# Moving half of a weight load behind the values of batch 1, and four half sums of weights into tile 1

## The chip, the core and the metric

The kernel runs on one core of a Trainium2 chip. A core has several engines that each work through a queue of their own: TensorE (PE in the profile) multiplies matrices, with a separate row, PEld, for loading the stationary operand; VectorE (DVE) and ScalarE (ACT) do elementwise work; GpSimd (POOL) does elementwise work more slowly and also issues most of the DMA transfers here; SyncE (SP) issues the others. An instruction starts when the one before it on its engine has gone and the semaphores that it waits for have been raised. The metric is the device time of one execution in microseconds (us).

## The reference

Attention in which keys and values are first averaged over groups of eight positions, followed by a two-layer network with a SiLU between its layers:

```python
k_p = k.reshape(B, H, Sp, pool, D).mean(axis=3)      # pool 8: 576 positions become 72
v_p = v.reshape(B, H, Sp, pool, D).mean(axis=3)
scores = scale * np.matmul(q, k_p.transpose(0, 1, 3, 2))
attn = softmax(scores)
x = np.matmul(attn, v_p)      # then to (4608 tokens, 512)
h = x @ w_in                  # 512 -> 2048
g = h * (1.0 / (1.0 + np.exp(-h)))
out = g @ w_out               # 2048 -> 512
```

There are 8 batches, 8 heads, 576 positions and a head dimension of 64. Inputs and output are float32; the kernel multiplies in bf16.

## The kernel before

The 4608 tokens are worked through in nine tiles of 512 (`NT`). For each tile the kernel needs the attention output `xT` and then two layers. Because 576 positions are not 512, a tile reaches into the next batch: tile 0's second half and tile 1 need keys and values of batch 1. While tile t is in its layers, the attention for tile t + 1 is worked in between.

From tile 1 on both layers (in tile 0 a part of the first) use Strassen's scheme, in the Winograd form: a 2 x 2 block product with seven multiplications instead of eight. It needs sums of blocks of both operands. Sums of w_in's blocks are `unit_weight_sum` (into `w_sum1`), of `xT` `unit_x_sum` (into `x_sum`), of w_out's blocks `weight_sum` (L841, into `w_sum`) and of the hidden layer `hidden_sum`. `weight_sum(n, i)` makes sum n (0 to 3) for half i of the rows; one call is one VectorE instruction that reads two operands from SBUF (L845, 128 x 1024 bf16). All eight calls have to be done before tile 1's second layer, which starts at 61.4 us. Tile 0 multiplies its second layer directly (`second_product`, L801): "m1:8-12" multiplies row block 1 of the hidden layer with blocks 8 to 11 of w_out's 16. It needs the DMA of just those blocks.

In tiles with the scheme a first-layer group (a, b, c, d) has products 1 to 7. "a6" is two steps of two matmuls each, followed by what `behind` (L916) does: after product 1 a copy of bank A into bank B, after product 5 a copy of bank E into f32, after product 6 the sum of bank B and that copy into bank E (L925, VectorE). Product 7 then adds into bank B, so it waits until that sum has read it.

The order is written by hand. A string such as `FIRST` (L1172, for tile 0) or `ONE` (L1177, for tile 1) gives TensorE's products in order; each is a number of steps, and `spread` (L682) issues other work at given steps: `at(86, select_v, 1, j)` puts the call behind step 86. Tile 0 has 108 steps. What stands under the same engine keeps the order in which it was issued, so a later number moves a call back in its engine's queue. The calls of tile 0 that matter here:

- `slot_sums` for "v" (L339): six VectorE additions (L346) that add the eight positions of a group for batch 1's values, in two parts, `raw` into `v5`. They wait for the three DMAs of `load_slots(nc.gpsimd, 1, "v", ...)`.
- `select_v` (L377): small matmuls that bring these sums into heads (`v_ps`, L386); `copy_v` (L411) copies them out on ScalarE; `turn_v` moves them with DMAs on SyncE.
- `denominators` and `reciprocals` (TensorE, then four ScalarE activations), `numerators` (L525, L501: TensorE), and `x_half` (L534, L537: four VectorE products into `xT`).
- `load_half_2`, `load_v_last`, `spread_keys`: loads and one small GpSimd operation for later tiles.

Tile 1 starts on VectorE with its four `unit_x_sum` (L735). `behind_x_sums` (L737) is a copy of one column of the last of these on GpSimd (`gate`, L738): GpSimd works in order, so what stands behind the copy there begins only after the x sums. Behind it stand six additions of batch 2's keys (`slot_sums` "k" with `eng=nc.gpsimd`), issued at tile 1's step 0.

All loads of w_in, w_out, q, and the k and v of batch 1 and later (but for `load_v_last`) go through one queue that GpSimd issues. `load_w_out(c, c1)` (L1052) loads eighths c up to c1 of w_out, two without c1; an eighth is two of the 16 blocks, 256 KB as it lands.

Of the kernel before, what the change touches and what calls it, by code (L numbers as in the profile page):

```python
# [36 lines left out]
def kernel(  # L37
# [9 lines left out]
    nc = tc.nc  # L47

    B, H, S, D = q.shape
# [144 lines left out]
    def last_rows(bs):  # L194

        lasts[bs] = mid.tile([128, 2, 2 * PH], FP32, tag="r_raw", bufs=1, name="r_raw")
        return lasts[bs][:, : len(bs)]
# [123 lines left out]
    def load_slots(eng, b, name, i0, i1, half=None):  # L321
        es = slice(0, RE) if half is None else slice(half * RE // 2, (half + 1) * RE // 2)
        src = (k if name == "k" else v)[b].rearrange("h (sp p) d -> (h sp) (p d)", p=POOL)
        src = src[:, es]
        how = dict(accum_op=ALU.add) if half else {}
        tiles = row_tiles[name]
        w = es.stop - es.start
        if i0 == SLOTS:
            eng.dma_start(
                out=tiles[1][:REST, SLOTS - SA, :w], in_=src[128 * SLOTS :], **how  # L330
            )
        else:
            j = i0 // SA
            eng.dma_start(
                out=tiles[j][:, i0 - SA * j : i1 - SA * j, :w],
                in_=src[128 * i0 : 128 * i1].rearrange("(i r) e -> r i e", r=128), **how
            )
# [714 lines left out]
    def load_w_out(c, c1=None):  # L1052
        cs = slice(c * KG // 8, (c + 2 if c1 is None else c1) * KG // 8)
        nc.gpsimd.dma_start(out=w_out_sb[:, cs, :], in_=w_out_r[:, cs, :])
# [73 lines left out]
    load_q(1, halves=True)  # L1128
    load_q_part(1, 0, 2 * UT - QI)
    load_w_out(3, 4)  # L1130
    load_w_out(4)
    load_slots(nc.gpsimd, 1, "v", 0, 3)
    load_slots(nc.gpsimd, 1, "v", 3, 4)
    load_slots(nc.gpsimd, 1, "v", 4, 5)
    load_w_out(6)
    row_masks(True)
    load_q_part(1, 2 * UT - QI, QI)
# [18 lines left out]
    def load_half_2(name, half):  # L1156
# [14 lines left out]
    )  # L1171
    FIRST = (  # L1172
        "p0.1 p2.1 c1 p4.1 c5 p6.1 c6 c2 d1 d5 c7 c3 d6 d2 c4 cs m0:0-2 d7 d3 m0:2-4 m1:0-1 ds d4"
        " m1:1-4 m2:0-4 m0:4-6 m1:4-6 m2:4-6 m0:6-8 m1:6-8 m2:6-8 m3:0-8 m0:8-12 m1:8-12 m2:8-12 m3:8-12 m0:12-16"
        " m1:12-16 m2:12-16 m3:12-16"
    )
    ONE = "a1 b1 a5 b5" + FOUR[FOUR.index(" a6"):].replace("o2:0-2", "o2:0-3").replace("o2:2-8", "o2:3-8")  # L1177
# [1 line left out]
    for t in range(NT):  # L1179
        a = t + 1  # L1180
        if t == 0:
            f = []

            def at(s, fn, *args, **kw):
                f.append((s, lambda: fn(*args, **kw)))

            for n in (0, 2, 1, 3):
                at(0, unit_x_sum, 0, n)
            for y, y_at in ((2, 0), (3, 18), (1, 66)):
                for n in range(4):  # L1190
                    at(y_at + n, unit_weight_sum, y, y + 1, n)
            for n in range(3):
                at((39, 42, 44)[n], slot_sums, "k", 0, levels=(n,))
            at(46, slot_sums, "k", 1)
            for a in range(2):
                at(50, q_transpose, 1, a, 0, QI - UT)
            for j in range(2):
                at(53, select_k, 1, j)
            at(53, copy_k, 1, slice(0, 2), nc.scalar.copy)
            for i0, i1 in ((0, SA), (SA, SLOTS), (SLOTS, SLOTS + 1)):  # L1200
                at(47, load_slots, nc.gpsimd, 2, "k", i0, i1)
            at(47, load_q, 2)
            for a in range(2):
                at(55 + a, q_transpose, 1, a, QI - UT, UT)
            at(52, attn_tables)
            for i in range(PW):
                at(63 + i, weight_sum, 0, i)
            for n in (1, 2, 3):
                at(74, weight_sum, n, 0)
            for j in range(2):  # L1210
                at(75 + j, slot_sums, "v", j)
                at(86, select_v, 1, j)
            at(86, copy_v, 1, 0, nc.scalar.copy, H)
            at(88, turn_v, 1)
            for n in (1, 2):
                at(91, weight_sum, n, 1)
            at(84, load_half_2, "v", 0)
            at(48, lambda: nc.gpsimd.memset(last_rows((1, 2))[:, :, :1], 0.0))
            at(80, load_v_last, 1, 2)
            at(84, spread_keys, 1, nc.gpsimd)  # L1220
            at(61, scores_half, 1, 0)
            at(73, scores_half, 1, 1)
            for n in range(2):
                at(84, denominators, 1, n)
                at(84, reciprocals, 1, n)
            at(92, numerators, 1, 0)
            at(92, numerators, 1, 1)
            for n in range(2):
                at(92, x_half, 1, n)
            at(93, moe_tables)  # L1230
            tile_products(0, FIRST, f)
            continue

        order = ORDER.get(t, FOUR if t < NT - 1 else BARE)
        if t == NT - 1:
            order = order.replace("P4 Q4", "R4 S4")
        o = 0
        f = []

        def at(s, fn, *args, **kw):  # L1240
            f.append((s, lambda: fn(*args, **kw)))

        def late(s, fn, *args, **kw):
            at(s + o, fn, *args, **kw)

        if t == 1:
            for n in (0, 2, 1, 3):
                at(0, unit_x_sum, 1, n)
            at(0, behind_x_sums)
        late(43, hidden_sum, 2, 0, 4)  # L1250
        late(53, hidden_sum, 2, 4, 8)
        late(64 if t < NT - 1 else 57, hidden_sum, 0, 0, 4)
        late(64 if t < NT - 1 else 62, hidden_sum, 1, 0, 4)
        late(65, hidden_sum, 0, 4, 8)
        late(66, hidden_sum, 1, 4, 8)
        late(76, hidden_sum, 3, 0, 8)
        if a < B:
            if t == 1:
                at(8, weight_sum, 3, 1)
                for j in range(2):  # L1260
                    at(0, slot_sums, "k", j, eng=nc.gpsimd)
                    at(42, select_k, 2, j)
                    at(43, copy_k, 2, j, nc.scalar.copy)
                    at(69, slot_sums, "v", j, halves=True)
                at(1, load_half_2, "v", 1)
                at(48, spread_keys, 2)
                at(84, pick_v, 2)
                for n in "kv":
                    at(3, load_one, 3, n)
                at(37, last_sums, 1, 2, eng=nc.vector, levels=(0,))  # L1270
                at(44, last_sums, 1, 2, eng=nc.vector, levels=(1, 2))
                at(46, load_v_last, 3)
                at(86, last_values, 1, 2, eng=nc.vector)
                for n in "kv":
                    at(5, load_rest, 3, n)
                at(33, load_q, 3)
            else:
                at(0, behind_x_sums)
                at(0, pool_k, a)
                if a + 1 < B:  # L1280
                    at(0, load_one, a + 1, "k")
                at(1, pool_v, a)
                if a + 1 < B:
                    at(1, load_one, a + 1, "v")
                    at(1, load_v_last, a + 1)
                    at(3, load_rest, a + 1, "k")
                    at(4, load_rest, a + 1, "v")
                    at(33, load_q, a + 1)
                at(34, k_transpose, a)
                at(35, spread_keys, a)  # L1290
        if t < NT - 1:
            tail = QI - UT + 2 * t
            for n in range(2):
                at((22, 32)[n], q_transpose, a, n, 0, tail)
                if tail < UT:
                    at((47, 55)[n], q_transpose, a, n, tail, UT)
            late(63, attn_tables)
            late(63, scores, a)
            late(88, sums_and_values, a)
            late(89, x_part, a, 0)  # L1300
            late(89, moe_tables)
            late(95, x_part, a, 1)
        if t < NT - 1:
            for n in (0, 2, 1, 3):
                late(102 if (t, n) == (1, 0) else 105, unit_x_sum, t + 1, n)
        tile_products(t, order, f, last=t == NT - 1)
# [28 lines left out]
```

## Time and profile before

| | us |
|---|---|
| three runs | 269.28, 269.98, 276.65 |
| median | 269.98 |
| the profiled execution, its own time | 269.99 |
| its span (first to last instruction) | 268.1 |
| second layer of tile 0: first product to last (L809) | 28.1 to 49.2 |
| tile 1's first product | 49.0 |

| DMA queue | packets | MB | share of 16 engines' span |
|---|---|---|---|
| issued by GpSimd (q0) | 22480 | 25.97 | 51.5% |
| hardware queues (q1) | 8384 | 11.87 | 16.6% |

The span lies 1.9 us below the execution's own time; sums are made against the latter. The granted TensorE clock is full over the whole span, and the DMA engines are busy in almost all of the first 50 us: in the stretches of 2 us from 16 to 44 us the mean share of the engines is 1.03 to 1.25 (packets overlap), with 195 to 397 GB/s. In a row of the timeline the columns are start, duration, engine, line, operation, what it writes and reads, shapes and count; in brackets the engine's idle time before it and what ended that. The ends of matmuls are modelled and overlap the next ones' starts, so a matmul's pace is read from starts.

### The profile page before, as it was taken

What the parts mean: (1) busy time and instruction counts of PE and PEld (TensorE: products, weight loads), DVE (VectorE), ACT (ScalarE), POOL (GpSimd) and SP (SyncE); (2) the same over time, 40 slices, a digit from 0 to 9 for tenths busy, and PEclk for the clock granted to TensorE, in tenths of its full rate; (3) what the DMA queues carried; (4) which work ended last, traced back from release to release, by engine and by line L of the source; (5) the groups of instructions that cost most, each with busy time, mean ns of one, the idle gap of its engine ahead of it and who ended that gap; (6) DMA issues with size and microseconds to landing.
All of it is one profiled execution on the core that took longest, in us unless ns stands there. A gap on an engine that the chain in (4) does not pass through costs nothing.

```text
span 268.1 us, 7721 instructions
## 1 busy us (share of the span) xinstructions
PE 261.0 (97%) x3143; PEld 212.4 (79%) x3148; DVE 209.8 (78%) x378; ACT 182.1 (68%) x319; POOL 114.9 (43%) x155
## 2 busy tenths in 40 slices
PE   8999998999999999999999999999999999999994
PEld 4468643788888888888888888888888887888883
DVE  4878978789797959895988598859886887686862
ACT  1579866788658865876587658765876677667700
POOL 8664745591638713872297229684900000000000
PEclk9999999999999999999999999999999999999999
DMA  7999999669698796579666956699500150015004
GB/s 208 284 205 288 205 284 299 204 141 202 134 163 223 205 184 129 134 173 182 131 154 161 182 121 155 148 177 125 120 12 0 37 125 0 2 32 127 2 0 157
DMA packets 31330, 38.97 MB, mean 145 GB/s; under 512 B 9760, under 2 KB 21536, under 8 KB 31296
## 3 DMA queue, kind: packets, MB, share of 16 engines
q0 software_dynamic: 22480, 25.97, 51.5%
q1 hardware_dynamic: 8384, 11.87, 16.6%
q10 hardware_dynamic: 432, 0.66, 0.7%
q8 instruction: 24, 0.39, 0.6%
q14 instruction: 10, 0.08, 0.1%
HBM read 37.88 MB, written 9.44 MB: 177 GB/s over the span
## 4 chain that ended last, share of the span: by engine, by line
PE 83%; DMA 13%; DVE 1%; issue 1%; POOL 0%; POOLq 0%
PE o_psB L910 16%; PE u_psB L891 16%; PE o_psA L910 11%; PE o_psE L910 11%; PE u_psE L891 10%; PE u_psA L891 10%; DMA raw<-in_k_dram 4%; DMA raw<-in_v_dram 4%; DMA w_in_sb<-in_moe_w_in_dram 3%; DMA q_bf<-in_q_dram 2%; PE o_ps L809 2%; PE sc_ps L575 2%; PE den_ps L604 1%; PE nu_ps L629 1%; DVE raw L346 1%
## 5 line engine op out<-in xcount | busy, mean ns | idle before, releaser
L891 PEld LDWEIGHTS <-w_sum 128*128 128x128 bf16 x544 | 52.8, 98 | 6.5
L910 PEld LDWEIGHTS <-h_sum 128*128 128x128 bf16 x512 | 48.8, 98 | 7.7 <-issue 0.4
L891 PEld LDWEIGHTS <-w_in_sb 128*128 128x128 bf16 x408 | 39.9, 98 | 4.8
L910 PEld LDWEIGHTS <-h_T 128*128 128x128 bf16 x384 | 36.9, 98 | 5.2 <-issue 0.4
L891 PE MATMUL u_psA<-xT,w_in_sb 128*128 128x256 bf16 x272 | 40.5, 273 | 0.0
L891 PE MATMUL u_psB<-x_sum,w_sum 128*128 128x256 bf16 x272 | 40.3, 273 | 0.1
L910 PE MATMUL o_psA<-w_out_sb,h_T 128*128 128x256 bf16 x256 | 32.1, 273 | 0.0
L910 PE MATMUL o_psB<-w_sum,h_sum 128*128 128x256 bf16 x256 | 31.8, 273 | 0.0
L925 DVE TENSOR_TENSOR u_psE<-u_psB,p 128x512 f32<-128x512 f32 x34 | 23.7, 697 | 8.7 <-PE u_psB L891 5.0
L929 ACT ACTIVATE h_T<-u_psE 128x512 bf16<-128x512 f32 x34 | 20.3, 597 | 10.2 <-PE u_psE L891 9.9
L942 DVE TENSOR_TENSOR c<-u_psB,p 128x512 f32<-128x512 f32 x34 | 23.2, 682 | 3.2 <-PE u_psB L891 2.1
L670 DVE TENSOR_TENSOR xT<-nu_ps,rec 128x512 bf16<-128x512 f32 x28 | 18.0, 682 | 9.8 <-ACT rec L654 9.8
L920 DVE COPY u_psB<-u_psA 128x512 f32<-128x512 f32 x30 | 20.8, 698 | 4.7 <-PE u_psA L891 4.2
L929 ACT ACTIVATE h_T<-u_psB 128x512 bf16<-128x512 f32 x34 | 20.4, 599 | 5.5 <-PE u_psB L891 5.5
L929 ACT ACTIVATE h_T<-u_psA 128x512 bf16<-128x512 f32 x34 | 20.5, 602 | 4.6 <-PE u_psA L891 4.5
L923 ACT COPY p<-u_psE 128x512 f32<-128x512 f32 x34 | 20.1, 595 | 4.0 <-PE u_psE L891 4.0
L211 POOL DMA_DIRECT2D v_raw<-in_v_dram x20 | 18.3, 1023 | 8.6 <-DMA v_raw<-in_v_dram 8.5
L929 ACT ACTIVATE h_T<-c 128x512 bf16<-128x512 f32 x34 | 21.7, 637 | 0.2 <-DVE c L942 0.2
L834 DVE TENSOR_TENSOR h_sum<-h_T 128x1024 bf16<-128x1024 bf16 x32 | 21.6, 679 | 0.2 <-ACT h_T L929 0.2
L834 DVE TENSOR_TENSOR h_sum<-h_T,h_sum 128x1024 bf16<-128x1024 bf16 (+1 forms) x24 | 20.7, 863 | 0.2
L891 PE MATMUL u_psB<-xT,w_sum 128*128 128x256 bf16 x136 | 20.4, 273 | 0.0
L891 PE MATMUL u_psE<-x_sum,w_in_sb 128*128 128x256 bf16 x136 | 20.4, 273 | 0.0
(125 smaller groups left out, 462.6 us busy)
## 6 DMA issues: line engine op xcount, KB each, us to landing
out_dram<-o_sb SPq DMA_DIRECT2D x128, 64.0 KB
raw<-in_k_dram POOLq DMA_DIRECT2D x10, 576.0 KB, 8.4
v_raw<-in_v_dram POOLq DMA_DIRECT2D x20, 256.0 KB, 7.5
q_bf<-in_q_dram POOLq DMA_DIRECT2D x5, 576.0 KB, 9.2
w_in_sb<-in_moe_w_in_dram POOLq DMA_DIRECT2D x8, 256.0 KB, 7.8
r_raw<-in_v_dram SPq DMA_DIRECT2D x28, 64.0 KB
raw<-in_v_dram POOLq DMA_DIRECT2D x2, 768.0 KB, 8.8
w_out_sb<-in_moe_w_out_dram POOLq DMA_DIRECT2D x3, 512.0 KB, 10.8
```

Of the source, the lines that this page charges most:

```text
L211: nc.gpsimd.dma_start(out=batches[b]["v_raw"][KM * g : KM * (g + 1)], in_=source(b, "v")[:KM, 4 * g : 4 * (g + 1), PH * half : PH * (half ...
L575: nc.tensor.matmul(sc[s][KM * g : KM * (g + 1), cs], lhsT=kz[b % 2][rows, g, c, :KM], rhs=qT[rows, g, us, :, c], start=(n == 0 and c == 0) ...
L670: nc.vector.tensor_mul(out=xT[:, 2 * g : 2 * g + 2, x_cols(t, f)], in0=st["nu"][g][f], in1=inv[:, f : f + 1, :].broadcast_to([128, 2, NQ]),)
L809: nc.tensor.matmul(ps["m", m], lhsT=h_T[:, g, m * 128 : (m + 1) * 128], rhs=w_out_sb[:, g, :], start=(g == 0), stop=(g == KG - 1),)
L834: nc.vector.tensor_tensor(out=h_sum[n][:, k0:k1, :], in0=get(a), in1=get(b), op=op)
L891: nc.tensor.matmul(ps[y, BANK[n]][:, u, :], lhsT=w[:, kk, 128 * u : 128 * (u + 1)], rhs=x[:, kk, :], start=n in (1, 5) and u == 0 and kk == 0,
L910: nc.tensor.matmul(o_bank(n, c), lhsT=left(n, kt, c), rhs=w[:, kt, :], start=n in (1, 5) and kt == 0 and c == 0, stop=kt == KQ - 1, skip_g ...
L920: (acopy if t == 0 or (t == 1 and y in (0, 1)) else vcopy)(ps[y, "B"], ps[y, "A"])
L923: acopy(f32[y], ps[y, "E"])
L925: tt(out=ps[y, "E"], in0=ps[y, "B"], in1=f32[y], op=add)
L929: nc.scalar.activation(h_T[:, g : g + 2, j * NQ : (j + 1) * NQ], src, func=AF.Silu)
L942: tt(out=c22, in0=ps[y, "B"], in1=f32[y], op=add)
```

## The change

Half of w_out's third quarter, eighth 5 (blocks 10 and 11), is loaded behind batch 1's values instead of before them, as a DMA of its own. Tile 0's second layer takes blocks 8 and 9 for all four row blocks first, and then blocks 10 and 11. Of the weight sums, `weight_sum(1, 0)` and `(2, 0)` go from step 74, ahead of the value sums, to step 89, behind them; `(3, 0)` and `(1, 1)`, `(2, 1)` leave tile 0 (steps 74 and 91) and stand with `(3, 1)` in tile 1 at step 1, behind the x sums. The selection of values, its copy and the moves behind it are issued four steps later, the denominators and reciprocals one step earlier, the numerators, products into `xT` and the table load behind them two steps later.

```diff
     load_w_out(3, 4)
-    load_w_out(4)
+    load_w_out(4, 5)
     load_slots(nc.gpsimd, 1, "v", 0, 3)
     load_slots(nc.gpsimd, 1, "v", 3, 4)
     load_slots(nc.gpsimd, 1, "v", 4, 5)
+    load_w_out(5, 6)
     load_w_out(6)
...
-        " m1:1-4 m2:0-4 m0:4-6 m1:4-6 m2:4-6 m0:6-8 m1:6-8 m2:6-8 m3:0-8 m0:8-12 m1:8-12 m2:8-12 m3:8-12 m0:12-16"
+        " m1:1-4 m2:0-4 m0:4-6 m1:4-6 m2:4-6 m0:6-8 m1:6-8 m2:6-8 m3:0-8 m0:8-10 m1:8-10 m2:8-10 m3:8-10 m0:10-12 m1:10-12 m2:10-12 m3:10-12 m0:12-16"
...
-            for n in (1, 2, 3):
-                at(74, weight_sum, n, 0)
+            for n in (1, 2):
+                at(89, weight_sum, n, 0)
             for j in range(2):
                 at(75 + j, slot_sums, "v", j)
-                at(86, select_v, 1, j)
-            at(86, copy_v, 1, 0, nc.scalar.copy, H)
-            at(88, turn_v, 1)
-            for n in (1, 2):
-                at(91, weight_sum, n, 1)
+                at(90, select_v, 1, j)
+            at(90, copy_v, 1, 0, nc.scalar.copy, H)
+            at(92, turn_v, 1)
...
             for n in range(2):
-                at(84, denominators, 1, n)
-                at(84, reciprocals, 1, n)
-            at(92, numerators, 1, 0)
-            at(92, numerators, 1, 1)
+                at(83, denominators, 1, n)
+                at(83, reciprocals, 1, n)
+            at(94, numerators, 1, 0)
+            at(94, numerators, 1, 1)
             for n in range(2):
-                at(92, x_half, 1, n)
-            at(93, moe_tables)
+                at(94, x_half, 1, n)
+            at(95, moe_tables)
...
             if t == 1:
-                at(8, weight_sum, 3, 1)
+                at(1, weight_sum, 3, 0)
+                for n in (1, 2, 3):
+                    at(1, weight_sum, n, 1)
```

## The prediction

> **What bounds the kernel now.** I read the busy shares first.
>
> ```profile
> PE 261.0 (97%) x3143; PEld 212.4 (79%) x3148; DVE 209.8 (78%) x378; ACT 182.1 (68%) x319; POOL 114.9 (43%) x155
> ```
>
> TensorE (PE) has work for all but some 7 us of the 268.1 us span. Whatever stops it adds to the end, and what removes a stop takes off the end; nothing later has slack to give back. The row of the granted clock is full throughout. Next, the waits between 41 and 50 us, the end of tile 0 (us in total, times, longest):
>
> ```profile
> PE v_ps L386 <- DVE v L346: 1.2, 2, 1.0
> ```
>
> This is the stop at which the change is made. TensorE's order around it and in the start of tile 1 (start, us, engine, line, what):
>
> ```profile
> 41.08 0.60 PE L809 MATMUL o_ps<-w_out_sb,h_T 128*128 128x512 bf16 x2
> 41.86 0.41 PE L386 MATMUL v_ps<-v,shifts 128*128 128x64 bf16 x8 [0.18 <-DVE v L346]
> 43.24 0.28 PE L386 MATMUL v_ps<-v,shifts 128*128 128x64 bf16 x4 [0.97 <-DVE v L346]
> ...
> 44.74 1.07 PE L501 MATMUL nu_ps<-es,vp 72*32 72x64 bf16 x48
> 45.97 3.18 PE L809 MATMUL o_ps<-w_out_sb,h_T 128*128 128x512 bf16 x14 [0.16 <-issue]
> 48.99 1.04 PE L891 MATMUL u_psA<-xT,w_in_sb 128*128 128x256 bf16 x8
> ...
> 52.49 0.60 PE L891 MATMUL u_psB<-x_sum,w_sum 128*128 128x256 bf16 x4
> ```
>
> Counted by starts, the stop is 1.4 to 1.5: two products from 41.08 fill until 41.5, eight small matmuls from 41.86 until 42.1 (the recorded ends hold a drain of 0.17). The row at 52.49 is product a7, which adds into the bank that VectorE's (DVE's) sum at 51.45 reads. On VectorE:
>
> ```profile
> 39.86 1.55 DVE L346 TENSOR_TENSOR raw<-raw 128x768 f32<-128x768 f32 x2 [0.94 <-DMA raw<-in_v_dram]
> ...
> 45.27 2.48 DVE L537 TENSOR_TENSOR xT<-nu_ps,rec 128x512 bf16<-128x512 f32 x4 [0.88 <-PE nu_ps L501]
> ...
> 49.39 0.68 DVE L845 TENSOR_TENSOR w_sum<-w_out_sb,w_sum 128x1024 bf16<-128x1024 bf16 x1
> 51.45 0.70 DVE L925 TENSOR_TENSOR u_psE<-u_psB,p 128x512 f32<-128x512 f32 x1 [1.38 <-PE u_psB L891]
> ```
>
> VectorE began batch 1's value sums when the load landed, so that stop starts in the DMA queue. Its DMAs (name, KB, us from issue to landing) were issued at 29.16, 31.27 and 31.81:
>
> ```profile
> w_out_sb<-in_moe_w_out_dram POOLq DMA_DIRECT2D x1, 512.0 KB, 7.8
> ...
> raw<-in_v_dram POOLq DMA_DIRECT2D x1, 128.0 KB, 9.6
> ...
> w_out_sb<-in_moe_w_out_dram POOLq DMA_DIRECT2D x1, 512.0 KB, 11.3
> ```
>
> They land one after the other: w_out's third quarter at 37.0, the last values at 40.9, w_out's last quarter at 43.1. Last, GpSimd (POOL) at the start of tile 1, and the gate copy's six durations (ns, least, median, most):
>
> ```profile
> 49.54 0.58 POOL L738 COPY gate<-x_sum 128x1 bf16<-128x1 bf16 x1 [4.35 <-DVE x_sum L735]
> 50.08 2.87 POOL L346 TENSOR_TENSOR raw<-raw 128x768 f32<-128x768 f32 x2
> ...
> L738 POOL COPY gate<-x_sum x6: 180/186/582, 49.5 to 186.6; 128x1 bf16<-128x1 bf16 x6
> ```
>
> The 582 ns one is this one. It ended at 50.12, just after the half sum that VectorE ran from 49.39 to 50.07; the others meet no such sum. The two engines exclude each other here, and the opposite order shows in tile 3 (VectorE's row, GpSimd's row, and all six of VectorE's):
>
> ```profile
> 113.12 0.63 DVE L279 TENSOR_TENSOR kzr<-kz,mask_k 128x128 bf16<-128x128 bf16 x1
> ...
> 112.88 1.25 POOL L254 TENSOR_TENSOR r_raw<-r_raw 128x256 f32<-128x256 f32 x2
> ...
> L279 DVE TENSOR_TENSOR kzr<-kz,mask_k x6: 251/394/634, 61.6 to 194.6; 128x128 bf16<-128x128 bf16 x6
> ```
>
> **The change part by part.** *The load.* The value loads pass 256 KB of w_out. The 512 KB took 37.0 - 34.1 = 2.9 us of the queue (the 256 KB load issued at 28.17 landed 5.9 us later, at 34.1), so half is 1.45 us: the values land at 38.4 to 39.5 instead of 39.8 to 40.9. The moved half lands where the last values did, 40.9; the last quarter stays at 43.1. One more issue costs GpSimd 0.7 us (its row at 28.17), hidden behind an issue-to-landing time of 8 to 11 us.
>
> *The half sums in tile 0.* Three left the place before the value sums and VectorE ends its earlier work at 36.2 (a row at 35.81 of 0.42), so the value sums (3.3 us, 39.86 to 43.19) run from 38.4 to 41.8. The two that come behind them last until 43.0, before VectorE is wanted again. They cost nothing.
>
> *TensorE's steps.* A step of m products is one matmul at 0.217 us (3.04 us for 14 from 45.97 on). Denominators move from 40.53 one step forward, to 40.31, and end 0.55 later, at 40.86. Then m0:10 meets the moved half at 40.9: no stop. Seven steps to 42.4, the selection of the values (0.4) to 42.8, long after 41.8: the stop is gone. One step, then m0:12 meets the last quarter at 43.1, and three steps end at 43.75. The numerators need ScalarE's copy of the values, which ended at 44.14 behind a chain from the denominators and so now at 43.92: start 43.95, end 44.9. Thirteen steps (two fewer than the 15 before, whose first has no row) put tile 1's first product at 47.75 instead of 48.99: **1.24 us gained**. Rows with nothing behind them: ScalarE's table load slips behind m0's copy, and its copies still catch up before a6; the bias of 0.2 either way goes into the range.
>
> *The four half sums in tile 1.* From the numerators' start VectorE needs 0.53 to its first product row and 4.12 more to the first half sum (45.27 to 49.39): 48.6. Four at 0.605 pitch (the half sums at 37.02 and 37.63) end at 51.0, the sum for a7 at 51.7. a7 is due 3.50 after the first product (48.99 to 52.49), at 51.25. So even undisturbed TensorE stops for 0.5 us here: VectorE's idle 1.38 before 51.45 covered less than three more.
>
> *GpSimd beside them.* Before, one half sum stood beside the gate copy, and the large additions of keys began as it ended. Now the gate comes at 48.7 into the first of four. No row shows a large GpSimd addition waiting between two half sums that follow each other. The bounds: 0 if VectorE keeps its turn through all four; 1.80 + 1.00 (the two parts of GpSimd's 2.87 at 50.08) if they alternate. I take alternation, because both rows end that way: the gate finished 0.05 after one VectorE instruction, and the 634 ns kzr 0.15 after one GpSimd addition though GpSimd had its next ready. Then: half sum 1 to 49.2, gate, half sum 2 to 49.9, addition of 1.80 to 51.65, half sum 3 to 52.25, addition of 1.00 to 53.2, half sum 4 to 53.8, the sum for a7 to 54.5. a7 stops 54.45 - 51.25 = 3.2 us. The instruction queued behind the blocked half sums is that sum; a7 and the whole of TensorE's queue wait for it.
>
> [...]
>
> Sum: 269.99 (the profiled execution; span 268.1 and 1.9 around it; the median of the three runs is 269.98) - 1.24 + 3.2 = **271.9 us**.
>
> **The rivals.** *VectorE keeps its turn.* The additions wait until 51.0; the four half sums cost only 0.5: 269.99 - 1.24 + 0.5 = 269.25, faster. For it: VectorE starts the next half sum 0.08 before the last is recorded as ended (pitch 0.605, duration 0.685), which may leave no opening. Against it: the kzr row, where the other engine's next addition was as close. It decides at 49.2: if the gate ends there and not at 51, it is false. The sign turns when the additions cost over 0.75 us.
>
> *One addition gets in, not two.* If the gate passes only after half sum 2, or half sum 4 wins over the second addition: 0.5 + 1.9 of stop, 271.1 to 271.2.
>
> *The moved half lands late.* If loads overtake each other and it lands nearer the last quarter (43.1 instead of 40.9), TensorE stops at m0:10 by up to 2.2: from 269.25 up to 271.5 with undisturbed half sums, and 274.2 with alternation. Against it: every landing here is in issue order. [...]
>
> *The values do not come earlier.* If the queue is not served in order, the stop stays and the half sums come on top: 270.5 to 273.2.
>
> **How the numbers follow.** Alternation 0.50 (271.9); VectorE keeps its turn 0.26 (269.25); one addition 0.16 (271.1); late half 0.05; values not earlier 0.03. The likeliest gives 271.9; its own range is 271.2 to 272.7, from 0.2 in ScalarE's copies, 0.3 in the landings and 0.2 in the 2.8 of additions. Both signs hold much of the chance, so the whole range reaches to the faster case less 0.4: 268.9 to 272.7. Two per cent of the time before is 5.4 us, about what a measurement of this kernel can tell from no change (its three runs spread 269.28 to 276.65). Only a late half together with both additions and more comes near it; no case gains as much, since the whole stop is 1.5. Faster 0.01, within 0.96, slower 0.03.
>
> **What would show it.** Right: no wait of v_ps for VectorE near 42; values landing near 38.4; first product of tile 1 near 47.75; the gate ended near 49.3; the 768-element addition of 1.8 us between two half sums, one half sum of over 2 us; a7 near 54.5. Wrong: half sums at even 0.605 pitch and GpSimd's additions starting near 51 (then 269.25); a stop of TensorE before m0:10 or m0:12 (then the landings); a7 without a stop.

## The result and the profile after

| | kernel before | changed kernel |
|---|---|---|
| median of 22 runs each, us | 270.86 | 272.96 |
| lowest to highest, us | 269.28 to 276.65 | 271.10 to 276.34 |
| ratio, with its 95% interval | | 1.0070 (1.0047 to 1.0093) |
| the profiled execution, us | 269.99 | 273.55 |
| its span, us | 268.1 | 271.8 |
| mean granted TensorE clock in it | 1.000 | 0.994 |

The change makes the kernel slower by some 2 us, well inside 2%. A few executions are over 1.5% slower than the fastest of their kernel; the ratios, here and below, leave them out and so are not the quotients of the medians. In the two profiled executions the difference is 3.6 us. The page of the changed kernel, its row of TensorE's share and its row of the clock:

```profile
PE 263.2 (97%) x3148; PEld 212.9 (78%) x3148; DVE 212.3 (78%) x378; ACT 181.8 (67%) x319; POOL 117.4 (43%) x156
...
PEclk9999999979999999999999999999999999999999
```

TensorE is busy 2.2 us longer with the same matmuls (each trace lacks a few records), and the clock, full before, has a slice at 7. TensorE's waits between 38 and 62 us (total, times, longest):

```profile
PE u_psB L891 <- DVE u_psE L925: 2.7, 1, 2.7
...
PE o_ps L809 <- DMA w_out_sb<-in_moe_w_out_dram: 0.3, 1, 0.3
```

The wait for the values is gone. A new one of 2.7 us is that of product a7. TensorE's timeline, from the end of tile 0 on:

```profile
41.18 1.67 PE L809 MATMUL o_ps<-w_out_sb,h_T 128*128 128x512 bf16 x7
42.69 0.51 PE L386 MATMUL v_ps<-v,shifts 128*128 128x64 bf16 x12
...
43.70 0.81 PE L809 MATMUL o_ps<-w_out_sb,h_T 128*128 128x512 bf16 x3 [0.28 <-DMA w_out_sb<-in_moe_w_out_dram]
44.44 1.07 PE L501 MATMUL nu_ps<-es,vp 72*32 72x64 bf16 x48
45.44 2.98 PE L809 MATMUL o_ps<-w_out_sb,h_T 128*128 128x512 bf16 x13
48.25 1.04 PE L891 MATMUL u_psA<-xT,w_in_sb 128*128 128x256 bf16 x8
...
54.66 1.01 PE L891 MATMUL u_psB<-x_sum,w_sum 128*128 128x256 bf16 x4 [2.74 <-DVE u_psE L925]
55.46 1.06 PE L891 MATMUL u_psE<-x_sum,w_in_sb 128*128 128x256 bf16 x4
...
57.96 0.60 PE L891 MATMUL u_psB<-xT,w_sum 128*128 128x256 bf16 x4
```

The twelve small matmuls at 42.69 run in one piece, and tile 1 begins at 48.25 instead of 48.99. Then a7, due 3.50 after that at 51.75, starts at 54.66. Behind it a group of four matmuls takes some 0.85 us from start to start, where it took 0.44, until 57.96. VectorE and GpSimd at the same place (start, us, engine, line):

```profile
39.05 1.55 DVE L346 TENSOR_TENSOR raw<-raw 128x768 f32<-128x768 f32 x2 [2.37 <-DMA raw<-in_v_dram]
...
49.09 1.29 DVE L845 TENSOR_TENSOR w_sum<-w_out_sb,w_sum 128x1024 bf16<-128x1024 bf16 x2
50.29 2.30 DVE L845 TENSOR_TENSOR w_sum<-w_out_sb 128x1024 bf16<-128x1024 bf16 x1
52.52 1.48 DVE L845 TENSOR_TENSOR w_sum<-w_out_sb,w_sum 128x1024 bf16<-128x1024 bf16 x1
53.92 1.28 DVE L925 TENSOR_TENSOR u_psE<-u_psB,p 128x512 f32<-128x512 f32 x2
```

```profile
49.23 0.58 POOL L738 COPY gate<-x_sum 128x1 bf16<-128x1 bf16 x1 [3.47 <-DVE x_sum L735]
49.77 3.67 POOL L346 TENSOR_TENSOR raw<-raw 128x768 f32<-128x768 f32 x2
```

The four half sums are 0.69, 0.69, 2.30 and 1.48 us long. The gate ends at 49.82, as the first half sum ends. GpSimd's first addition then waits for the second half sum (2.27 us from 49.77 on, where it took 1.80 before), and the third half sum waits for that addition. The two additions together took 2.87 before and take 3.67 now. The sum that a7 needs ends at 54.60. The loads around the values, issued at 29.34, 31.39, 31.93 and 32.65 (KB, us to landing):

```profile
w_out_sb<-in_moe_w_out_dram POOLq DMA_DIRECT2D x1, 256.0 KB, 7.0
...
raw<-in_v_dram POOLq DMA_DIRECT2D x1, 128.0 KB, 8.8
...
w_out_sb<-in_moe_w_out_dram POOLq DMA_DIRECT2D x1, 256.0 KB, 9.2
...
w_out_sb<-in_moe_w_out_dram POOLq DMA_DIRECT2D x1, 512.0 KB, 11.0
```

They land at 36.4, 40.2, 41.1 and 43.7, in issue order (the first is w_out's eighth 4, the third the moved half); the first values land at 39.0, where VectorE's sums start. Last, the engines and the clock in three stretches of 3.41 us (busy PE, PEld, DVE, ACT, POOL with counts, the granted clock, DMA share, GB/s):

```profile
51.05:54.47 3.42, 0.86 (x8) 0.62 (x7) 3.42 (x3) 1.34 (x3) 3.26 (x4) 1.00 0.44 141
54.47:57.88 3.41, 3.23 (x16) 2.23 (x16) 1.89 (x4) 0.60 (x1) 3.21 (x5) 0.50 0.54 132
57.88:61.30 3.42, 3.42 (x33) 3.07 (x32) 2.24 (x6) 3.14 (x7) 3.42 (x6) 1.00 0.86 141
```

In the stretch after the stop TensorE is granted half its clock, for 3.41 us and no longer. It worked in 3.2 us of that stretch, so half of this, 1.6 us, is lost. The whole difference of spans is 3.7 us, and three terms give it to within 0.1: -0.74 (earlier start of tile 1) + 2.91 (a7 against its due time) + 1.6 (half clock).

### The profile page after: what moved, and what is told of

Same layout as the page of the kernel before. It is cut to its first block, busy times and chain, and to the rows that moved or that the text cites. A ratio compares the mean times of both kernels' runs of the same rounds, so it can differ in the third digit from the quotient of the medians.

```text
span 271.8 us, 7728 instructions
## 1 busy us (share of the span) xinstructions
PE 263.2 (97%) x3148; PEld 212.9 (78%) x3148; DVE 212.3 (78%) x378; ACT 181.8 (67%) x319; POOL 117.4 (43%) x156
## 4 chain that ended last, share of the span: by engine, by line
PE 81%; DMA 12%; POOL 3%; issue 1%; DVE 1%; POOLq 0%; DVEq 0%
PE u_psB L891 16%; PE o_psB L910 16%; PE o_psA L910 11%; PE u_psE L891 11%; PE o_psE L910 10%; PE u_psA L891 10%; DMA raw<-in_k_dram 5%; DMA w_out_sb<-in_moe_w_out_dram 4%; DMA w_in_sb<-in_moe_w_in_dram 3%; PE sc_ps L575 2%; PE den_ps L604 1%; PE o_ps L809 1%; PE nu_ps L629 1%; POOL raw L334 1%; POOL q_bf L132 1%
## 5 line engine op out<-in xcount | busy, mean ns | idle before, releaser
L891 PE MATMUL u_psB<-x_sum,w_sum 128*128 128x256 bf16 x272 | 41.2, 277 | 2.7 <-DVE u_psE L925 2.7
L891 PE MATMUL u_psE<-x_sum,w_in_sb 128*128 128x256 bf16 x136 | 21.2, 281 | 0.0
```

What stands on the lines that cost most here:

```text
L891: nc.tensor.matmul(ps[y, BANK[n]][:, u, :], lhsT=w[:, kk, 128 * u : 128 * (u + 1)], rhs=x[:, kk, :], start=n in (1, 5) and u == 0 and kk == 0,
```

## The experiments

Two theories were to be kept apart. *Collision*: VectorE's half sums and GpSimd's additions of keys hold each other up in turn, and a7 waits behind them. *Clock*: behind the stop TensorE then works for a stretch at half clock, which costs more time. The rivals stand with each run. Times are compared with the kernel before on the same chip.

**GpSimd's additions behind the half sums.** A second gate copy, from the last half sum, stands ahead of them.

```diff
                 at(1, weight_sum, 3, 0)
                 for n in (1, 2, 3):
                     at(1, weight_sum, n, 1)
+                at(1, lambda: nc.gpsimd.tensor_copy(out=gate, in_=w_sum[:, 3, KQ - 1, CQ - 1 :]))
+                for j in range(2):
+                    at(1, slot_sums, "k", j, eng=nc.gpsimd)
...
                 for j in range(2):
-                    at(0, slot_sums, "k", j, eng=nc.gpsimd)
```

> The changed kernel, but GpSimd's six additions of batch 2's keys start only when tile 1's last half sum of weights has ended. Collision (VectorE's half sums and GpSimd's additions hold each other up, which makes the stop before a7): four half sums at a pitch of about 0.6 us, none over 0.75, a7 stopped by 0.2 to 0.6 us instead of 2.9, no stretch at half clock, and a time of 0.1 to 0.7 us under the kernel before. Rival (four half sums are too many in this place, whatever GpSimd does): a7 still stopped by over 2 us and the time stays some 2 us over the kernel before.

Measured: 269.54 us against 270.29, ratio 0.9971 (0.9940 to 1.0002), the profile's span 267.0. VectorE's timeline of this kernel, then GpSimd's, then TensorE's row of a7:

```profile
48.19 1.28 DVE L845 TENSOR_TENSOR w_sum<-w_out_sb,w_sum 128x1024 bf16<-128x1024 bf16 x2
49.39 0.68 DVE L845 TENSOR_TENSOR w_sum<-w_out_sb 128x1024 bf16<-128x1024 bf16 x1
49.99 0.68 DVE L845 TENSOR_TENSOR w_sum<-w_out_sb,w_sum 128x1024 bf16<-128x1024 bf16 x1
50.60 1.29 DVE L925 TENSOR_TENSOR u_psE<-u_psB,p 128x512 f32<-128x512 f32 x2
```

```profile
50.81 0.19 POOL L1261 COPY gate<-w_sum 128x1 bf16<-128x1 bf16 x1 [1.89 <-DVE w_sum L845]
50.94 2.89 POOL L346 TENSOR_TENSOR raw<-raw 128x768 f32<-128x768 f32 x2
```

```profile
51.34 0.60 PE L891 MATMUL u_psB<-x_sum,w_sum 128*128 128x256 bf16 x4 [0.33 <-DVE u_psE L925]
```

The same four half sums, none blocked: the pitch is 0.60, GpSimd's additions are back at 2.89 us, and a7 waits 0.33. So GpSimd's work between them makes the long half sums, and through them nearly all of the stop. The time is 0.3% under that of the kernel before, in an interval that just includes no difference.

**The half sums alone.** The kernel before, with only the three half sums moved.

```diff
-            for n in (1, 2, 3):
+            for n in (1, 2):
                 at(74, weight_sum, n, 0)
...
-            for n in (1, 2):
-                at(91, weight_sum, n, 1)
...
-                at(8, weight_sum, 3, 1)
+                at(1, weight_sum, 3, 0)
+                for n in (1, 2, 3):
+                    at(1, weight_sum, n, 1)
```

> The kernel before, with only the three half sums of weights moved into tile 1 behind the x sums; loads and steps as before. Collision: the stop before the values (1.4 us) stays, one half sum of over 2 us, a7 stopped by 2.5 to 3.2 us, 2.5 to 4.5 us over the kernel before (the upper end where the clock halves after the stop). Rival (the moved load and steps cost the time, the half sums little): within 0.6 us of the kernel before.

Measured: 274.64 us against 270.29, ratio 1.0122 (1.0086 to 1.0157). The profile has the stop before the values as before, half sums of 0.69, 0.69, 2.30 and 1.48, and a7 stopped by 2.3 us (2.5 against its due time). Its waits between 38 and 60 us:

```profile
PE u_psB L891 <- DVE u_psE L925: 2.3, 1, 2.3
PE v_ps L386 <- DVE v L346: 1.3, 2, 1.0
```

The moved half sums alone lose more than the whole change does (1.2% against 0.7%). Taking one of them, (3, 0), from ahead of the value sums did nothing for the wait for the values: VectorE still begins those sums when the load lands, at 40.16. In this profiled execution the clock stayed full after the stop. That is the rarer case: four of the twelve executions have a mean clock of 0.997 or more and a median of 272.8 us, the other eight 0.987 to 0.994 and 275.2. Two stretches of 3.41 us that meet inside the stop, same columns as above:

```profile
50.77:54.18 3.41, 2.19 (x21) 1.81 (x19) 3.41 (x3) 2.48 (x5) 3.25 (x3) 1.00 0.48 149
54.18:57.60 3.42, 2.33 (x22) 2.09 (x22) 3.15 (x6) 0.99 (x2) 3.26 (x4) 1.00 0.56 141
```

Each of the two holds over 2 us of TensorE's work, and the clock is 1.00 in both.

**The loads and steps alone.** The changed kernel with one half sum in tile 1, as before.

```diff
-            for n in (1, 2):
+            for n in (1, 2, 3):
                 at(89, weight_sum, n, 0)
+            for n in (1, 2):
+                at(93, weight_sum, n, 1)
...
-                at(1, weight_sum, 3, 0)
-                for n in (1, 2, 3):
-                    at(1, weight_sum, n, 1)
+                at(8, weight_sum, 3, 1)
```

> The changed kernel, with its loads and steps, but only one half sum in tile 1 as before; the other three stay in tile 0 behind the value sums. Collision: no stop before the values, none before a7, no half clock, 0.5 to 1.2 us under the kernel before. Rival (loads and steps cost): a stop before m0:10 or m0:12 of over 1 us and a time at or over the kernel before.

Measured: 269.02 us against 270.29, ratio 0.9936 (0.9912 to 0.9960), span 266.5, first product of tile 1 at 47.46, no stop before m0:10, m0:12 or a7. The median gain, 1.3 us, is just above the 0.5 to 1.2 expected. So the loads and steps, the other half of the change, are a gain of 0.4 to 0.9%; this run does not part the two from each other.

**Matmuls in the stop.** The changed kernel with TensorE kept busy while it waits.

```diff
+                def fill(n):
+                    bank = ps_tile([128, 512], FP32, "at", "fill_ps")
+                    for _ in range(n):
+                        nc.tensor.matmul(bank, lhsT=warm[:, :128], rhs=warm, start=True, stop=True)
+
+                at(15, fill, 12)
```

> The changed kernel, with 12 matmuls of zeros (2.6 us at full clock, into a free bank, not used) put ahead of a7 in TensorE's queue. Clock (the stop leaves TensorE idle long enough that it is granted half its clock for 3.4 us afterwards, worth 1.6 us): a7 starts when it did (2.9 us late), its matmuls and those behind keep the pace of 0.109 us, no stretch at half clock, and the profile's span is 1.4 to 1.8 us under that of the changed kernel (271.8). Rival (the slow matmuls behind a7 wait for something else): they stay at 0.21 us and the time stays.

Measured: 271.70 us against 270.29, ratio 1.0044 (1.0013 to 1.0076), span 269.7, clock 1.0. TensorE's timeline (one of the twelve added matmuls has no record):

```profile
51.21 2.75 PE L1264 MATMUL fill_ps<-warm 128*128 128x512 bf16 x11
54.12 0.60 PE L891 MATMUL u_psB<-x_sum,w_sum 128*128 128x256 bf16 x4 [0.15 <-DVE u_psE L925]
54.55 0.60 PE L891 MATMUL u_psE<-x_sum,w_in_sb 128*128 128x256 bf16 x4
```

a7 is as late as it was, 6.4 us after the first product (47.72 to 54.12), but what follows keeps its pace of 0.44 a group. The span is 2.1 us under that of the changed kernel, more than the 1.4 to 1.8 expected, because tile 1 here began 0.5 us earlier. Eleven of its twelve runs have a mean clock of 0.998 or more.

**Three half sums, two half sums.** The changed kernel again, with (3, 0), and then with (3, 0) and (1, 1), left in tile 0.

```diff
-            for n in (1, 2):
+            for n in (1, 2, 3):
                 at(89, weight_sum, n, 0)
+            at(93, weight_sum, 1, 1)
...
-                at(1, weight_sum, 3, 0)
-                for n in (1, 2, 3):
+                for n in (2, 3):
                     at(1, weight_sum, n, 1)
```

(This is the edit for two; for three, the line at step 93 is missing and tile 1 keeps n = 1, 2, 3.)

> The changed kernel with three half sums in tile 1 instead of four; (3, 0) stays in tile 0 behind the value sums. Collision by turns (gate after the first, the large key addition after the second): the third half sum takes 2.2 to 2.4 us and no other over 0.75; a7 stops by 1.2 to 1.8 us; no half clock; between 0.5 us under and 0.8 over the kernel before. Rival (each half sum costs its own time, about a fourth of the stop): stop of 2.1 us and a time about 1 us over.

> The changed kernel with two half sums in tile 1; (3, 0) and (1, 1) stay in tile 0. Collision by turns: the key addition begins only after the second half sum, so both take 0.69 us, a7 does not stop, and the time is that of the kernel with one half sum there, 0.5 to 1.7 us under the kernel before. Rival (each half sum costs): a stop of some 0.7 to 1.4 us at a7 and a time at or over the kernel before.

Measured: with three, 269.98 us against 270.90, ratio 0.9977 (0.9955 to 0.9999); with two, 268.69 us, ratio 0.9938 (0.9913 to 0.9964). VectorE's timeline with three, from the third half sum, and TensorE's row of a7:

```profile
49.63 2.30 DVE L845 TENSOR_TENSOR w_sum<-w_out_sb,w_sum 128x1024 bf16<-128x1024 bf16 x1
51.85 1.28 DVE L925 TENSOR_TENSOR u_psE<-u_psB,p 128x512 f32<-128x512 f32 x2
```

```profile
52.59 0.60 PE L891 MATMUL u_psB<-x_sum,w_sum 128*128 128x256 bf16 x4 [1.34 <-DVE u_psE L925]
```

And with two, VectorE's:

```profile
48.28 0.68 DVE L845 TENSOR_TENSOR w_sum<-w_out_sb 128x1024 bf16<-128x1024 bf16 x1
48.88 0.68 DVE L845 TENSOR_TENSOR w_sum<-w_out_sb,w_sum 128x1024 bf16<-128x1024 bf16 x1
50.03 1.44 DVE L925 TENSOR_TENSOR u_psE<-u_psB,p 128x512 f32<-128x512 f32 x2 [0.47 <-ACT p L923]
```

Both are faster than expected: by the medians three are 0.9 us under the kernel before (0.5 under to 0.8 over was expected) and two are 2.2 under (0.5 to 1.7), in a set in which eight of the kernel before's 21 executions have a mean clock of 0.991 to 0.994. The price is not a share with each half sum: TensorE does not wait at a7 with one or two, 1.34 us with three and 2.74 with four. With two, GpSimd's first addition begins behind the second half sum and VectorE still idles before the sum for a7; with three, exactly one half sum is blocked. The turns that fit all these profiles are half sum, gate, half sum, addition, half sum, addition, half sum.

**The changed kernel again, and the kernel before with its stop filled.** The second is the kernel before with `at(86, fill, 6)` (the same `fill`) ahead of `select_v`.

> The changed kernel once more, on the chip of these runs. Collision: third half sum 2.3 us, a7 2.6 to 3.0 us late. Clock: the half-rate stretch of 3.4 us stands in some executions and not in others, so the profile's span is either about 271 to 272 with it or 269.5 to 270.5 without it, and the times spread over more than 2 us; median 1.5 to 2.8 us over the kernel before and 0.4 to 1.2 over the kernel with the 12 matmuls (which was 1.4 over). Rival (the half clock is there each time): all times within 1 us, 3 to 3.6 us over.

> The kernel before with 6 matmuls of zeros (1.3 us, not used) ahead of the selection of the values, where TensorE stops. Clock (in some of its executions the kernel before too loses clock after this stop, which is what lifts its median to 270.9 from the 270.0 of the executions at full clock): the mean granted clock is 0.997 or more in nearly all executions, the times lie within about 0.8 us, median 269.8 to 270.4 and 0.3 to 1.0 under the kernel before. Rival (the lower clocks of the kernel before come from elsewhere): about two in five executions still show a clock of 0.994 or less and the median is that of the kernel before.

Measured, changed kernel: 273.05 us against 270.90, ratio 1.0083 (1.0046 to 1.0119), span 271.8, with a mean clock of 0.994 as in the first. Each run lists its mean granted clock, and with it the times part: of the 22 runs of the first comparison, eight with 0.998 or more have a median of 271.6 us, thirteen with 0.991 to 0.994 one of 273.1 (one more, at 276.34, has 0.988). Here it is three at 271.3 to 272.3 and four at 273.1 to 273.8. So executions that lose clock take 1.5 to 1.8 us more, and they are about six in ten.

Measured, filled kernel before: 269.98 us against 270.27, ratio 0.9982 (0.9963 to 1.0001), all twelve runs at a clock of 0.997 or more. Of the 22 runs of the kernel before beside it, five have 0.991 to 0.994 and a median of 271.4, the other seventeen 270.0. That speaks for the 1.4 us stop before the values as what costs clock in some executions, but does not prove it: at five in 22, twelve executions would show none by chance about one time in twenty. Over all sets whose clocks are listed, 20 of 78 executions of the kernel before lie below 0.997, and 3 of 67 of the kernels in which no stop of over 1 us is left unfilled; but the kernel with three half sums, with a stop of 1.3 us, has none in ten. The gain in time, 0.3 us of the median, is at the low end of what was expected and not clear of zero, and the times spread over 1.25 us, not 0.8.

**Two half sums again**, the same kernel in another set of runs.

> The changed kernel with two half sums in tile 1, once more: 268.3 to 269.2 us in nearly all executions, 0.4 to 0.9% under the kernel before; clock 0.997 or more in all. If the first run's gain was luck of its chip: within 0.3% of the kernel before.

Measured: 269.10 us against 270.27, ratio 0.9952 (0.9925 to 0.9980), 268.39 to 270.59; one run of twelve has a clock of 0.993. Only seven of the twelve lie in the 268.3 to 269.2 expected for nearly all, but the gain holds: 0.2 to 0.8% under the kernel before, while the changed kernel was over it in both of its sets.

## Why the prediction was right and where it was wrong

The direction and the collision were right, the time was not: 271.9 (268.9 to 272.7) was forecast and 272.96 measured, because the sum had no term for the clock. Point by point:

- *The load.* Right. The values landed at 39.0 to 40.2 in this profile (forecast 38.4 to 39.5), after w_out's eighth 4 and ahead of the moved half, which came in at 41.1. Over the eight profiles with the new order of loads the value sums begin at 38.5 on average, over the three with the old at 40.0: 1.4 us earlier, as forecast. The stop before the values is gone in every profile with the new order of loads.
- *TensorE's steps.* "1.24 us gained" was 0.74 in this profile: the last quarter landed at 43.7 instead of 43.1 and m0:12 waited 0.28, m0:10 some 0.2. Over all profiles here the first product of tile 1 lies at 47.36 to 48.25 with the new loads (eight profiles, mean 47.8) and at 48.99 to 49.30 without (three, mean 49.1). The term is right to 0.2 on the average; the starts in single profiles spread by 0.9 us with the new loads.
- *Four half sums undisturbed cost 0.5.* Measured 0.33 where they were undisturbed (additions behind them).
- *GpSimd beside them.* Right, by alternation: "the gate ended near 49.3; ... one half sum of over 2 us" came as gate at 49.82 and 2.30 us; the stop forecast at 3.2 was 2.9. The second addition held the fourth half sum up by 0.79 (1.48 - 0.69), not the 1.00 that was added for it.
- *The rivals.* VectorE does not keep its turn: GpSimd's waiting instruction gets in although VectorE's next half sum has been started 0.09 before the last one's end (the third starts at 50.29, the second ends at 50.38, the addition ends at 52.04). In the profiles of both kernels the loads around the values land in issue order: w_out, the last values and w_out at 37.0, 40.9 and 43.1 before, and at 36.4, 40.2, 41.1 and 43.7 after, where the moved half comes third.

The step that failed is the one under "what bounds the kernel now": "The row of the granted clock is full throughout". The sum then has 269.99 - 1.24 + 3.2 and no term for the clock, as if a stop of 3 us that the change brings left the clock as it was without that stop. It did not: TensorE was granted half its clock for 3.41 us behind the stop, 1.6 us more in the profiled execution and 1.5 to 1.8 in six of ten. Filling the stop took it away (eleven of twelve executions at 0.998 or more). In the sum's own terms the profiled execution is 269.99 - 0.74 + 2.91 + 1.6 = 273.8, against 273.55 measured. At full clock the changed kernel takes 271.6, near the forecast; the range, which ended at 272.7, had nothing in it for the others.

A smaller slip of the same kind: 269.99 is an execution at full clock. Where clocks are listed, the kernel before takes 270.0 to 270.3 at full clock, and 270.3 to 270.9 as the median of all; the clocks of the 22 executions behind its 270.86 are not listed. That the two medians differ by 2.1 us, close to the 1.96 that the sum gives, is therefore partly luck: at full clock the change costs 1.3 to 1.6, because it gains 1.3 on average at the start of tile 1 and loses 2.9, not 3.2, at a7.

The blocked half sums agree with one another: the third one took 2.30 us in the profiles of the changed kernel, of the half sums alone, with the stop filled and with three, which is its own 0.69 and 1.6 of an addition that took 1.80 in the kernel before. Not every GpSimd instruction held a half sum up for as long as it ran: the one at 33.36 in the kernel before stood beside a GpSimd multiplication of 0.87 us (33.19 on) and took 774 ns, where the median of its kind is 688. Who comes next when both have work queued, the runs with two, three and four half sums answer for this place: they alternate (0.68 and 0.68; 0.68, 0.68 and 2.30; 0.69, 0.69, 2.30 and 1.48 us).

## What to carry to other kernels

Work moved behind a critical chain on VectorE was not paid by its own duration here, where GpSimd had long two-input additions released at the same point (half sums of 0.69 us became 2.30 and 1.48 beside additions of 1.80 and 1.00): count the instructions that would alternate, and put the additions behind the last of them, or move no more there than run before the first addition gets its turn (two here). Where a change brings a stop of TensorE of two or three microseconds, price the clock after it as well, and expect it in a part of the executions only (here the clock was lower in 18 of 29, worth 1.5 to 1.8 us by the medians, with a stop of 2.7 in the profile). When a change has two halves, price and run each alone: here the loads and steps were worth 0.4 to 0.9%, and the half sums took that and more.

## What the runs showed of the hardware

In the changed kernel's profiled execution the granted clock is 1.00 up to 54.47, 0.50 from there to 57.88, 3.41 us, and 1.00 behind that. In the 3.42 us ahead of the fall (51.05 to 54.47), which hold most of the stop of 2.74, TensorE worked for 0.86 us. The second profiled execution of this kernel has the same span of 271.8 and the same mean clock of 0.994. In the profile of the half sums alone, with a stop of 2.31, the clock is 1.00 in both stretches of 3.41 us that meet at 54.18 inside the stop, with 2.19 us of work in the one and 2.33 in the other. Why the half clock followed in the one profile and not in the other is not shown.

By the listed clocks, 18 of 29 executions of the changed kernel, with a stop of 2.74 us in its profile, have a mean clock of 0.994 or less, and so have eight of twelve with the half sums alone (2.31) and one of twelve with the stop filled; with three half sums (1.34) the ten lie at 0.997 or more. How long a stop must be is not shown beyond that.

What costs clock in the kernel before (5 of 22, 8 of 21 and 7 of 35 executions) stays open. In its profile the stretch that holds the 1.4 us stop (40.97 to 44.39) has 2.27 us of TensorE's work and a clock of 1.00. No profile caught one of the executions with the lower clock.
